# Gated scan and feed-forward on one core: second unit's spreads split between two queues, state copies on another engine, new order

## The chip, the cores and the metric

One core of a Trainium2 chip runs the whole program. The metric is the device time of one execution in microseconds. TensorE, VectorE, ScalarE, GpSimd and SyncE run their own instruction streams and wait for each other by semaphores; in the views they are PE (its weight loads PEld), DVE, ACT, POOL and SP. SP computes nothing here: it issues transfers.

## The reference

For 4 batches and 8 heads, a state of 48 x 48 complex numbers is decayed by a gate and fed with k and v at each of 768 steps; y is read out with q. The rows of y, 3072 tokens of 384, then go through a feed-forward layer of 2048 with a piecewise quadratic gate.

```python
for t in range(S):
    ar, ai = (a_re_n[:, :, t, :, None], a_im_n[:, :, t, :, None])
    new_re = ar * S_re - ai * S_im
    new_im = ar * S_im + ai * S_re
    kv = np.einsum('bhd,bhe->bhde', k[:, :, t], v[:, :, t])
    S_re, S_im = (new_re + kv, new_im)
    y[:, :, t] = np.einsum('bhd,bhde->bhe', q[:, :, t], S_re)
...
h = x @ w_in
g = np.where(pos, h, np.where(neg, 0.0, (h + beta) ** 2 / (4.0 * beta)))
return (g @ w_out).astype(np.float32)
```

(a_re_n and a_im_n are the gates, scaled to a size below 1; pos and neg are h >= 1 and h <= -1.)

## The kernel before

The tokens are cut into 12 units of 256 (3 of each batch), and a unit into 2 chunks of 128. Each unit passes through two stages. `gates(u)` makes running sums of the logarithms and angles of the gates (logarithm, exponential, arctangent and sine on ScalarE, the rest on VectorE; for units 0 and 1 the sums are matmuls of TensorE), multiplies k and q with them (the tile `kq`, and `x`: the "turn", two instructions of VectorE for units 0 and 1), and sends the two results from their rows to rows sorted by head: `spread`, five transfers for `x` and five for `kq`, into three tiles `hd0`, `hd1` (three heads each) and `hd2` (two heads). `attend(u)` then takes each chunk through visits of TensorE: the scores of all heads into two PSUM tiles, which VectorE masks into `am0` and `am1` (copy under a mask, "masked copy"); the transposes of k, which ScalarE copies to `kT`; the values (`am` times `V`, plus state times q from the second chunk on), which ScalarE copies to `xr`; and the products of k and v, which go to the state `st`. When a unit's values stand in `xr`, six small transfers move rows of two heads within it. `split` makes the two parts `xH` (ScalarE) and `xL` (VectorE) of `xr`, and `moe` runs the feed-forward part over a block of two units: `gemm1(f)` into `h`, the gate on ScalarE and VectorE (`s`, `g`, `gh`, `gl`), `gemm2(f)`. The first two f of block 0 run on one unit at a time. Each matmul of it is done three times, on upper and lower parts. The weights are decoded on the way: `raw_i` and `raw_o` are loaded, and VectorE and ScalarE make upper and lower parts; for the first three tiles TensorE forms the lower one (`rest`).

The order of the work is not found at run time: every operation is recorded with its engine and its cost, and `ORDER`, a written table of 2324 numbers, says in which order all are emitted. Each engine then runs its own in that order. `Plan.order` works out planned times from the costs; they are used for one thing only, the number of filler matmuls (`idle`) that `warm` puts ahead of a TensorE operation where the plan has a gap, up to the first one of `moe`. What an instruction waits for is found from the tiles that it reads and writes when it is emitted, not from the plan. Transfers take eight semaphores in turn, over all queues together; a transfer that takes a semaphore again waits until the one that had it before has landed.

In `attend`, `visit` records the parts of a visit one after the other, and the first of them carries what all of them read:

```python
last = pl.op("PE", cost, run, r=reads if n == 0 else r, w=[psum], glue=last)
```

In `gates`, `spread(g, e, t)` takes its engine from a table of which no unit makes use (`SPREADS = 0`), so SP issues all:

```python
eng = SPREAD[e] if u < SPREADS else "SP"
```

e = 1 is the spread of `x` and e = 0 that of `kq`, which comes second.

Of the kernel before, what the change touches and what calls it, by code (L numbers as in the profile page):

```python
# [15 lines left out]
ALU = mybir.AluOpType  # L16
# [7 lines left out]
HR = 2 * D  # L24
# [40 lines left out]
    0, 1, 11, 2, 192, 201, 219, 210, 42, 3, 28, 4, 106, 12, 151, 5, 13, 14, 6, 193, 7, 194, 15, 8,  # L65
    16, 195, 9, 17, 196, 10, 18, 197, 202, 20, 19, 198, 203, 21, 26, 22, 211, 24, 23, 27, 212, 25,
    30, 35, 204, 34, 213, 31, 220, 32, 46, 29, 45, 33, 221, 199, 38, 40, 47, 39, 225, 41, 48, 97,
    54, 36, 44, 49, 43, 98, 51, 50, 55, 52, 53, 99, 200, 57, 100, 60, 101, 56, 37, 102, 103, 61, 58,
    205, 59, 104, 107, 206, 62, 105, 65, 66, 214, 113, 63, 207, 64, 152, 208, 111, 226, 118, 222,
    153, 114, 227, 110, 154, 112, 67, 228, 223, 109, 69, 209, 68, 116, 229, 155, 71, 115, 73, 72,  # L70
    117, 215, 70, 74, 108, 230, 156, 75, 231, 224, 157, 237, 77, 166, 76, 158, 79, 81, 78, 159, 80,
    83, 160, 85, 119, 86, 161, 82, 216, 121, 84, 162, 87, 232, 164, 163, 95, 233, 165, 120, 88, 123,
    238, 125, 124, 92, 122, 126, 89, 239, 168, 127, 90, 167, 513, 129, 94, 128, 169, 93, 131, 130,
    91, 133, 170, 132, 540, 234, 135, 137, 136, 217, 134, 138, 171, 235, 139, 141, 297, 218, 240,
    140, 149, 142, 172, 241, 143, 173, 144, 298, 175, 146, 174, 236, 145, 305, 176, 317, 147, 306,
    242, 299, 318, 177, 148, 307, 300, 243, 96, 301, 329, 249, 541, 178, 308, 319, 302, 186, 320,
    303, 180, 542, 321, 309, 304, 179, 543, 310, 341, 311, 181, 188, 322, 312, 342, 182, 150, 323,
    244, 519, 330, 313, 245, 189, 343, 324, 187, 331, 314, 190, 246, 315, 353, 523, 325, 250, 354,
    517, 247, 316, 355, 191, 326, 332, 338, 183, 248, 327, 184, 340, 333, 544, 516, 365, 334, 185,
    328, 339, 545, 255, 251, 350, 518, 344, 522, 335, 351, 546, 515, 252, 366, 336, 514, 509, 547,  # L80
    345, 520, 511, 253, 337, 521, 346, 510, 363, 548, 254, 352, 356, 347, 364, 261, 549, 367, 348,
    555, 357, 524, 256, 526, 824, 550, 349, 362, 527, 512, 525, 374, 368, 551, 528, 358, 369, 257,
    554, 530, 359, 529, 532, 370, 258, 534, 371, 259, 533, 376, 553, 552, 262, 377, 360, 260, 378,
    557, 263, 379, 267, 389, 361, 372, 390, 531, 558, 264, 388, 380, 559, 375, 373, 381, 560, 387,
    265, 391, 382, 399, 392, 383, 536, 561, 393, 538, 401, 268, 394, 562, 402, 537, 556, 384, 386,
    564, 403, 563, 385, 400, 565, 395, 412, 566, 266, 413, 396, 269, 411, 273, 404, 414, 567, 405,
    415, 270, 406, 571, 398, 574, 397, 271, 410, 573, 407, 422, 416, 572, 568, 425, 417, 575, 569,
    423, 408, 578, 825, 272, 426, 577, 579, 424, 409, 539, 580, 427, 570, 418, 576, 434, 274, 279,
    826, 436, 419, 428, 275, 435, 429, 437, 276, 827, 438, 535, 277, 439, 828, 581, 420, 278, 829,
    280, 285, 830, 589, 421, 598, 582, 281, 591, 601, 430, 602, 831, 593, 440, 595, 431, 603, 447,  # L90
    832, 590, 604, 449, 441, 592, 605, 450, 833, 442, 597, 606, 608, 599, 443, 451, 600, 834, 282,
    444, 448, 596, 607, 835, 432, 461, 609, 446, 586, 283, 462, 585, 433, 838, 463, 587, 594, 837,
    584, 459, 286, 445, 891, 841, 610, 287, 836, 284, 842, 612, 611, 288, 291, 452, 614, 839, 843,
    464, 613, 616, 615, 289, 844, 460, 453, 618, 620, 619, 472, 617, 454, 471, 621, 845, 465, 455,
    622, 624, 846, 466, 290, 623, 892, 632, 292, 625, 467, 847, 626, 840, 458, 456, 630, 473, 848,
    631, 474, 583, 468, 457, 849, 475, 868, 293, 627, 485, 476, 850, 588, 486, 893, 294, 483, 856,
    628, 487, 852, 477, 857, 470, 478, 469, 858, 295, 484, 479, 855, 482, 851, 636, 629, 634, 496,
    871, 296, 480, 494, 861, 488, 481, 495, 859, 489, 853, 498, 854, 638, 490, 873, 637, 499, 635,
    894, 860, 497, 862, 491, 642, 895, 639, 863, 650, 492, 896, 877, 640, 651, 870, 493, 897, 643,
    878, 641, 500, 633, 875, 898, 876, 501, 899, 872, 502, 874, 503, 864, 900, 505, 869, 866, 507,  # L100
    865, 504, 901, 506, 879, 508, 867, 881, 880, 652, 902, 882, 644, 908, 903, 968, 904, 883, 645,
    646, 885, 884, 647, 653, 887, 648, 654, 889, 906, 655, 658, 907, 888, 659, 890, 910, 669, 649,
    660, 909, 656, 670, 661, 668, 911, 657, 666, 662, 667, 912, 905, 663, 678, 913, 664, 671, 680,
    672, 665, 681, 914, 677, 673, 682, 915, 679, 683, 674, 691, 916, 688, 675, 917, 692, 684, 918,
# [1686 lines left out]
```

## Time and profile before

| | us |
|---|---|
| median of 3 runs | 556.41 (556.22 to 556.45) |
| the profiled execution | 555.64 |
| its span, first to last instruction | 553.7 |
| PE busy | 543.3 |
| DVE busy | 434.0 |
| ACT busy | 390.2 |

The profiled execution is shorter than the median by 0.77 us; 1.94 us of it lie outside the span. All times in the rows are counted from the start of the span. The granted clock of TensorE was 1.00 in all 40 slices of the page. Idle time of DVE and ACT costs something only where PE waits behind it.

### The profile page before, as it was taken

Reading aid. Unit: us, or ns where it says so; the run is one execution under the profiler, and the core shown is the slowest. Engines: PE = TensorE matmul, PEld = TensorE weight load, DVE = VectorE, ACT = ScalarE, POOL = GpSimd, SP = SyncE. Lnnn points to the kernel's source line nnn. Section 1 sums busy time; section 2 is a strip of 40 time slices with the busy share of each in tenths; the row PEclk is TensorE's granted clock in tenths of the full one; section 3 lists DMA queues with packets and bytes.
Section 4 is the critical chain, followed back from the end, with each engine's and each line's share of the span. In section 5 each row is a group of like instructions: output and inputs, shape, how many; then the busy total and the mean of one; then the engine's idle time right before and its main releaser. Section 6 shows DMA issues by size and latency. Waiting matters only on the chain.

```text
span 553.7 us, 10884 instructions
## 1 busy us (share of the span) xinstructions
PE 543.3 (98%) x4255; PEld 459.0 (83%) x4255; DVE 434.0 (78%) x631; ACT 390.2 (70%) x634; POOL 4.1 (1%) x27
## 2 busy tenths in 40 slices
PE   7999999999999999999999999999999999999997
PEld 7878878888888888888888888888888888888885
DVE  6999999999899798896977887776887476454553
ACT  7896899989966767666755776555753455577875
POOL 2000000000000000000000000000000000000000
PEclk9999999999999999999999999999999999999999
DMA  8776564465451342542411532421534510077751
GB/s 343 305 209 250 193 199 186 122 210 185 135 195 52 87 141 70 188 126 76 156 57 47 181 114 54 165 60 37 187 98 120 179 56 9 24 262 240 265 178 60
DMA packets 28487, 80.58 MB, mean 146 GB/s; under 512 B 6160, under 2 KB 13200, under 8 KB 28432
## 3 DMA queue, kind: packets, MB, share of 16 engines
q1 hardware_dynamic: 28288, 79.72, 43.4%
q8 instruction: 34, 0.56, 0.4%
q14 instruction: 21, 0.17, 0.1%
q10 hardware_dynamic: 144, 0.13, 0.1%
HBM read 55.05 MB, written 4.72 MB: 108 GB/s over the span
## 4 chain that ended last, share of the span: by engine, by line
PE 87%; DVE 6%; ACT 2%; DMA 2%; issue 1%; SPq 1%; ACTq 0%; DVEq 0%
PE o L1371 36%; PE h L1294 35%; PE at L1119 5%; PE at L1163 3%; PE at L1171 3%; PE at L1091 2%; PE at L1062 2%; DMA ai<-in_art_dram 1%; SPq L474 1%; DVE kq L828 1%; DVE kq L962 1%; DMA xr<-xr 1%; DVE x L962 1%; ACT ai L690 1%; DVE x L711 0%
## 5 line engine op out<-in xcount | busy, mean ns | idle before, releaser
L1371 PE MATMUL o<-gh,wo 128*128 128x512 f32 x576 | 178.9, 392 | 0.0
L1294 PE MATMUL h<-xH,wi 128*128 128x512 f32 (+1 forms) x576 | 177.4, 389 | 0.3 <-DVE g L1338 0.2
L1371 PEld LDWEIGHTS o<-gh,wo 128*128 128x128 f32 x576 | 106.5, 188 | 22.2 <-issue 0.2
L1294 PEld LDWEIGHTS h<-xH,wi 128*128 128x128 f32 x576 | 105.7, 188 | 22.7 <-DVE g L1338 1.5
L1371 PE MATMUL o<-gl,wo 128*128 128x512 f32 x288 | 112.0, 389 | 0.0
L1294 PE MATMUL h<-xL,wi 128*128 128x512 f32 (+1 forms) x288 | 111.4, 387 | 0.2 <-DVE xL L1269 0.2
L1319 ACT ACTIVATE s<-h,cst 128x512 f32<-128x512 f32 x94 | 64.4, 687 | 59.7 <-PE h L1294 38.7
L1338 DVE TENSOR_TENSOR g<-h,s 128x512 f32<-128x512 f32 x94 | 64.7, 689 | 50.9 <-ACT s L1319 49.2
L1356 DVE TENSOR_TENSOR gl<-g,gh 128x512 fp32r<-128x512 f32 x96 | 65.9, 687 | 25.8 <-ACT gh L1352 25.0
L1352 ACT CAST gh<-g 128x512 fp32r<-128x512 f32 x96 | 59.1, 616 | 28.1 <-DVE g L1346 18.5
L1294 PEld LDWEIGHTS h<-xL,wi 128*128 128x128 f32 x288 | 54.1, 188 | 11.8 <-DVE xL L1269 0.6
L1371 PEld LDWEIGHTS o<-gl,wo 128*128 128x128 f32 x288 | 54.0, 188 | 11.4
L1346 DVE SCALAR_TENSOR_TENSOR g<-s,g 128x512 f32<-128x512 f32 x80 | 54.9, 687 | 1.2
L690 ACT ACTIVATE ai<-ai 128x768 f32<-128x768 f32 (+1 forms) x48 | 40.5, 846 | 10.9 <-DVE ai L704 5.4
L1131 DVE COPY_PREDICATED am<-tri,at 128x512 f32<-128x512 uint32 x44 | 32.4, 741 | 8.2 <-PE at L1119 8.1
L1119 PE MATMUL at<-hd 96*64 96x128 f32 (+1 forms) x704 | 35.8, 248 | 0.1
L773 DVE TENSOR_TENSOR_SCAN ai<-again,ai 128x768 f32<-128x768 uint8 x20 | 35.1, 1753 | 1.0 <-ACT ai L690 0.9
L1119 PEld LDWEIGHTS at<-hd 96*64 96x64 f32 x704 | 33.4, 137 | 1.2 <-issue 0.7
L1171 PE MATMUL at<-am,V 128*64 128x128 f32 x352 | 33.1, 273 | 0.1
L1163 PE MATMUL at<-hd,st 96*64 96x128 f32 x304 | 30.7, 278 | 0.0
L483 ACT ACT_TABLE_LOAD x23 | 29.5, 1283 | 0.4
L1068 ACT COPY kT<-at 128x384 f32<-128x384 f32 x36 | 16.8, 478 | 11.0 <-PE at L1062 10.9
(137 smaller groups left out, 650.6 us busy)
## 6 DMA issues: line engine op xcount, KB each, us to landing
chk<-in_wl_dram SPq DMA_DIRECT2D x16, 768.0 KB, 5.6
kq<-in_kq_dram SPq DMA_DIRECT2D x12, 768.0 KB, 6.2
ai<-in_ari_dram SPq DMA_DIRECT2D x10, 768.0 KB, 5.3
V<-in_v_dram SPq DMA_DIRECT2D x12, 576.0 KB, 5.4
raw_i<-in_wl_dram SPq DMA_DIRECT2D x8, 768.0 KB, 5.0
raw_o<-in_wl_dram SPq DMA_DIRECT2D x8, 768.0 KB, 5.6
hd<-kq SPq DMA_DIRECT2D x40, 144.0 KB, 2.3
hd<-x SPq DMA_DIRECT2D x40, 144.0 KB, 2.4
```

Of the source, the lines that this page charges most:

```text
L690: lambda: A_.activation(out(), src(), f, **kw),
L773: lambda: V_.tensor_tensor_scan(dst().rearrange("p j t -> p (j t)"), again, src().rearrange("p j t -> p (j t)"), 0.0, op0=ALU.mult, op1=AL ...
L1119: PE_.matmul(SC.get()[o : o + HC, i + e, HC * k :], chunk(h, c, 0, HC * k)[:, :HC], chunk(h, c, 1, HC * k), start=True, stop=True,)
L1163: PE_.matmul(o_, st.get().rearrange("p h e -> p (h e)")[:, lo : lo + 64], chunk(h, c, 1), start=True, stop=False,)
L1171: PE_.matmul(o_, V.get()[:, c, lo : lo + 64], ams[pr // 2].get()[:, 2 * (pr % 2) + e, :], start=st is None, stop=True,)
L1294: PE_.matmul(H.get()[:, lo:hi], weight["i", f // 2].get()[:, f % 2, part, sl], x.get()[:, j, lo:hi], start=j == 0 and n == 0, stop=j == NJ ...
L1319: lambda: A_.activation(SS.get(), H.get(), AF.Relu, bias=c_half, scale=-0.5 if spare else 0.5),
L1338: lambda: V_.tensor_tensor(G.get(), H.get(), SS.get(), op=ALU.max),
L1346: lambda: V_.scalar_tensor_tensor(G.get(), SS.get(), 1.0, G.get(), op0=ALU.min, op1=ALU.mult),
L1352: pl.op("ACT", act(T), lambda: A_.copy(GH.get(), G.get()), r=[G], w=[GH])
L1356: lambda: V_.tensor_tensor(GL.get(), G.get(), GH.get().bitcast(F32), op=ALU.subtract),
L1371: PE_.matmul(LAST.get() if half else PO[m].get()[:, ts], weight["o", f // 2].get()[:, f % 2, part, sl], g.get()[:, ts], start=(f == NF - h ...
```

## The change

Five transfers of unit 1 (the spreads of `kq`) are issued by ScalarE instead of SP. The first copy of each batch's state from PSUM is done by ScalarE instead of VectorE. For unit 0 each part of a visit is recorded with its own reads alone. The table `ORDER` is another one throughout.

```diff
-SPREADS = 0
-SPREAD = ("SP", "ACT")
...
-            eng = SPREAD[e] if u < SPREADS else "SP"
+            eng = "ACT" if u == 1 and not e else "SP"
...
             def tail():
                 if old is None:
-                    fn = lambda: V_.tensor_copy(ST.get(), DP.get()[:HR])
-                else:
-                    fn = lambda: V_.tensor_tensor(ST.get(), old.get(), DP.get()[:HR], op=ALU.add)
-                pl.op("DVE", dve(DM), fn, r=[DP] + ([old] if old else []), w=[ST])
+                    pl.op(
+                        "ACT",
+                        act(DM, psum=True),
+                        lambda: A_.copy(ST.get(), DP.get()[:HR]),
+                        r=[DP],
+                        w=[ST],
+                    )
+                    return
+                pl.op(
+                    "DVE",
+                    dve(DM),
+                    lambda: V_.tensor_tensor(ST.get(), old.get(), DP.get()[:HR], op=ALU.add),
+                    r=[DP, old],
+                    w=[ST],
+                )
...
-                last = pl.op("PE", cost, run, r=reads if n == 0 else r, w=[psum], glue=last)
+                last = pl.op("PE", cost, run, r=reads if n == 0 and u else r, w=[psum], glue=last)
...
 ORDER = [
-    0, 1, 11, 2, 192, 201, 219, 210, 42, 3, 28, 4, 106, 12, 151, 5, 13, 14, 6, 193, 7, 194, 15, 8,
...
+    0, 1, 11, 2, 192, 210, 201, 28, 106, 3, 219, 4, 42, 12, 151, 5, 13, 14, 6, 193, 7, 194, 15, 8,
...
```

All 2324 places of the table are open to the change; three of them matter to the text below.

The first place is the issue of unit 1's spreads. In SP's list before, all ten stand in a row behind unit 0's, `x` and `kq` mixed (line 474 is the issue of a transfer; `hd_364`, `hd_386` and `hd_356` are unit 1's three tiles, `x_157` and `kq_148` its `x` and `kq`; the semaphores named are those that a transfer waits for).

```order
L474 DMA hd_356<-x_157 16x512 [waits DMAHW7_49,DVE_49]
L474 DMA hd_356<-kq_148 16x512 [waits DMAHW0_49,DVE_49]
L474 DMA hd_364<-kq_148 48x1536 [waits DMAHW1_49]
L474 DMA hd_356<-x_157 32x1024 [waits DMAHW2_49]
L474 DMA hd_356<-x_157 16x512 [waits DMAHW3_49]
L474 DMA hd_386<-x_157 48x1536 [waits DMAHW4_49]
L474 DMA hd_356<-kq_148 32x1024 [waits DMAHW5_49]
```

In SP's list now (L472), only the five of `x` stand there, behind a weight load (L486; unit 1's tiles are now `hd_370`, `hd_385` and `hd_373`), and the first of them waits for semaphore 2, which ScalarE's first transfer has.

```order
L486 DMA raw_i_360<-in_wl_dram 128x1536 [waits DMAHW1_49,PE_49]
L472 DMA hd_370<-x_157 48x1536 [waits DMAHW2_49,DVE_49]
L472 DMA hd_373<-x_157 16x512 [waits DMAHW3_49]
L472 DMA hd_385<-x_157 48x1536 [waits DMAHW5_49]
L472 DMA hd_373<-x_157 32x1024 [waits DMAHW7_49]
L472 DMA hd_373<-x_157 16x512 [waits DMAHW1_49]
```

In ScalarE's list now, the five of `kq` stand between its computing instructions, two together and three one by one among the copies of `kT` (L1066), `xr` (L1192) and the state (L1102); L688 is a gate instruction, and the fifth follows one `kT` copy behind the last row shown.

```order
L472 DMA hd_370<-kq_155 48x1536 [waits DVE_49]
L472 DMA hd_385<-kq_155 48x1536 [waits DMAHW5_49]
L525 CAST wo_398<-raw_o_256 128x2x384 [waits DMAHW3_49,DVE_49]
L688 ACTIVATE ai_159<-ai_159 128x768 [waits DVE_49]
L1066 COPY kT_93<-at_111 128x384 [waits PE_49]
L1066 COPY kT_94<-at_109 128x384 [waits DVE_49,PE_49]
L688 ACTIVATE ai_159<-ai_159,cst 128x768 [waits Activation_49]
L1192 COPY xr_444<-at_110 128x4x128 [waits DVE_49,PE_49]
L472 DMA hd_373<-kq_155 16x512 [waits DMAHW4_49]
L1102 COPY st_466<-at_111 96x384 [waits PE_49]
L688 ACTIVATE x_351<-x_351,cst 128x768 [waits DVE_49]
L472 DMA hd_373<-kq_155 32x1024 [waits DMAHW6_49]
```

The second place is TensorE behind the transposes of unit 0's second chunk (L1062 is a transpose, L1119 a score, L1163 and L1171 the values). Before, the scores of unit 1 (`hd_1`) come next, and unit 0's values behind them.

```order
L1062 MATMUL at0_109<-ident_64,hd0_121 128x96
L1062 MATMUL at0_109<-ident_64,hd1_122 128x96
L1062 MATMUL at0_109<-ident_64,hd2_123 128x96 x2
L1119 MATMUL o0_112<-hd_1_364 64x128
L1119 MATMUL o0_112<-hd_1_386 64x128
```

Now unit 0's values follow (L1172 and L1180), then its products, and only then unit 1's scores.

```order
L1060 MATMUL at0_109<-ident_64,hd0_121 128x96
L1060 MATMUL at0_109<-ident_64,hd1_122 128x96
L1060 MATMUL at0_109<-ident_64,hd2_123 128x96 x2
L1172 MATMUL at1_110<-hd0_121,st_0_466 64x128
L1172 MATMUL at1_110<-hd1_122,st_0_466 64x128
L1180 MATMUL at1_110<-am0_82,V_0_260 64x128 x2
```

The third place is VectorE from the turns of unit 1 (L962, `x_1` and `kq_1`) to the masked copies of unit 0's first chunk (L1131). Before, the weight instructions (L503, L521, L512) stand behind both turns, and a gate instruction of unit 2 (L704) between the masked copies.

```order
L962 TENSOR_TENSOR kq_0_152<-kq_0_152,ai_0_135 128x1536
L962 TENSOR_TENSOR x_1_157<-kq_1_148,ai_1_137 128x1536
L962 TENSOR_TENSOR kq_1_148<-kq_1_148,ai_1_137 128x1536
L503 TENSOR_SCALAR y_o1_358<-raw_o1_270 128x768
L521 SCALAR_TENSOR_TENSOR raw_i2_144<-raw_i2_144 128x768
L512 SCALAR_TENSOR_TENSOR raw_o1_270<-raw_o1_270,y_o1_358 128x768
L521 SCALAR_TENSOR_TENSOR raw_o1_270<-raw_o1_270 128x768
L1131 COPY_PREDICATED am0_82<-tri_69,at0_109 128x512
L704 TENSOR_TENSOR ai_2_159<-ai_2_159 128x768
L1131 COPY_PREDICATED am1_83<-tri_69,at1_110 128x512
```

Now a weight instruction stands ahead of each turn of unit 1, and the two masked copies follow each other.

```order
L960 TENSOR_TENSOR kq_0_146<-kq_0_146,ai_0_135 128x1536
L510 SCALAR_TENSOR_TENSOR raw_o1_256<-raw_o1_256,y_o1_312 128x768
L960 TENSOR_TENSOR x_1_157<-kq_1_155,ai_1_137 128x1536
L519 SCALAR_TENSOR_TENSOR raw_i2_152<-raw_i2_152 128x768
L960 TENSOR_TENSOR kq_1_155<-kq_1_155,ai_1_137 128x1536
L519 SCALAR_TENSOR_TENSOR raw_o1_256<-raw_o1_256 128x768
L702 TENSOR_TENSOR ai_2_159<-ai_2_159 128x768
L1140 COPY_PREDICATED am0_82<-tri_69,at0_109 128x512
L1140 COPY_PREDICATED am1_83<-tri_69,at1_110 128x512
```

The same instructions stand there in both but for the places named; the masked copies of unit 0's second chunk follow each other now too, and in unit 1's first chunk a weight instruction (L519) stands between them.

## Rows read from the trace of the kernel before

**Rows 1.** Two stretches: busy us of each engine, granted clock, DMA share, GB/s.
```profile
30.00:50.00 20.00, 18.44 (x273) 16.18 (x273) 19.83 (x25) 16.21 (x25) 0.00 (x0) 1.00 0.79 263
70.00:545.00 475.00, 475.00 (x3565) 399.21 (x3566) 366.89 (x529) 330.22 (x548) 0.00 (x0) 1.00 0.40 130
```

**Rows 2.** TensorE in order of time: start, us, engine, line, what [idle before].
```profile
36.00 2.13 PE L1119 MATMUL at<-hd 96*64 96x128 f32 x32
...
39.98 1.09 PE L1171 MATMUL at<-am,V 128*64 128x128 f32 x16
...
44.94 1.57 PE L1119 MATMUL o<-hd 96*64 96x128 f32 x31 [0.71 <-DMA hd<-x]
46.33 0.29 PE L1163 MATMUL at<-hd,st 96*64 96x128 f32 x1
...
49.18 0.88 PE L1062 MATMUL o<-ident,hd 96*128 96x96 f32 x8
...
50.46 1.09 PE L1171 MATMUL o<-am,V 128*64 128x128 f32 x16
...
58.54 1.16 PE L1441 MATMUL idle<-tri,ident 128*128 128x128 f32 x8
...
60.36 0.40 PE L1294 MATMUL h<-xH,wi 128*128 128x256 f32 x2
...
60.72 0.40 PE L1294 MATMUL h<-xH,wi 128*128 128x256 f32 x2
...
67.46 0.62 PE L1294 MATMUL at<-xH,wi 128*128 128x512 f32 x2
...
68.14 0.62 PE L1294 MATMUL at<-xH,wi 128*128 128x512 f32 x2
...
69.90 0.73 PE L1294 MATMUL h<-xH,wi 128*128 128x512 f32 x2 [0.24 <-DVE g L1338]
```

**Rows 3.** VectorE in order of time, same columns.
```profile
32.79 1.76 DVE L962 TENSOR_TENSOR kq<-kq,ai 128x1536 f32<-128x1536 f32 x1
...
39.20 0.73 DVE L1131 COPY_PREDICATED am<-tri,at 128x512 f32<-128x512 uint32 x1
...
49.41 0.73 DVE L1131 COPY_PREDICATED am<-tri,o 128x512 f32<-128x512 uint32 x1
...
54.93 0.74 DVE L1131 COPY_PREDICATED am<-tri,o 128x512 f32<-128x512 uint32 x1
...
59.13 0.95 DVE L1269 TENSOR_TENSOR xL<-xr,xH 128x768 fp32r<-128x768 f32 x1
```

**Rows 4.** ScalarE in order of time, same columns.
```profile
48.52 0.56 ACT L1183 COPY xr<-at 128x512 f32<-128x512 f32 x1
...
57.39 0.83 ACT L1262 CAST xH<-xr 128x768 fp32r<-128x768 f32 x1 [1.25 <-DMA xr<-xr]
```

**Rows 5.** The tiles hd, 27 to 50 us: issues min/median/max ns, landing.
```profile
L474 SPq DMA_DIRECT2D hd<-kq x10: 514/588/1430, 31.0 to 40.2; - x10
...
DMA to landing us min/median/max: 2.2/3.2/4.1
```

**Rows 6.** The end: issues of the output (ns), and ScalarE's copies.
```profile
L474 SPq DMA_DIRECT2D out_dram<-ob x2: 394/394/395, 548.1 to 549.1; - x2
L474 ACTq DMA_DIRECT2D out_dram<-ob x1: 381/381/381, 548.6 to 548.6; - x1
547.46 1.64 ACT L1412 COPY ob<-o 128x512 f32<-128x512 f32 x3 [1.71 <-PE o L1371]
```

**Rows 7.** SP's waits in all: us, times, longest.
```profile
SPq L474 <- DMA hd<-kq: 9.8, 5, 3.7
```

**Rows 8.** Transfers issued in the first 62 us: KB, median us to landing.
```profile
hd<-kq SPq DMA_DIRECT2D x4, 32.0 KB, 2.5
```

**Rows 9.** Copies out of PSUM by line: busy us, mean ns | idle before.
```profile
L1101 DVE COPY st<-at 96x384 f32<-96x384 f32 x3 | 1.6, 546 | 0.2 <-PE at L1091 0.2
L1068 ACT COPY kT<-at 128x384 f32<-128x384 f32 x36 | 16.8, 478 | 11.0 <-PE at L1062 10.9
```

268 rows, old and new, of the table ORDER are left out of this document.

## The prediction

> **What bounds the kernel now.** I read the stretches first, then TensorE in order of time, and then who it waited for. From 70 to 545 us TensorE is busy for 475.00 of 475.00 us at the granted clock 1.00, the upper of its two levels (2.4 GHz) [rows 1]; the reader is to see that nothing done there on another engine can show as time, unless it opens a gap. Both orders hold the same matmuls: 2043 of the feed-forward part, 1241 of gates and attention, 12 of the weights' rests; only the fillers go from 80 to 76, and they stand in idle time. So the end moves by as much as the last idle moment before 70 us moves. That is the first group of gemm1 for f = 4, at 69.90, behind a wait of 0.24 us for a `g` of VectorE [rows 2].
>
> Ahead of it lies the prologue. There TensorE waits, and these are the places [rows 2]: scores of unit 0 from 36.00 for 2.13 us, though the same 32 matmuls take 1.57 us at 44.94; 0.71 us before 44.94 for spreads of unit 1; fillers until 50.46; fillers from 58.54 until the feed-forward part starts; and then a first group that ends only at 60.36, because `xL` is made from 59.13 to 60.08 [rows 3]. From 60.36 to 69.90 there are 9.54 us for 11 groups of 256 columns (0.36 us each, 60.36 to 60.72) and 6 of 512 (0.68 us, 67.46 to 68.14): 3.96 + 4.08 = 8.04 us of work, 1.50 us of waiting [rows 2].
>
> VectorE is full in that time (19.83 of 20 us between 30 and 50), ScalarE is not (16.21 of 20) [rows 1]. ScalarE stands 1.25 us before it makes `xH` at 57.39, waiting for the moves `xr<-xr` [rows 4].
>
> **Part by part.**
>
> *The waits of unit 0's visits.* The line changes what the planner believes, not what an instruction waits for. In the order before, the first matmul of the scores already waits for hd0's and the second for hd1's transfers, and only the ones on hd2 for hd2's; in the trace the scores start at 36.00 and stretch. So the edit by itself is worth 0; it acts through the table alone. No cover is needed for it.
>
> *VectorE up to the first values.* The values of unit 0's first chunk start at 39.98, right behind the second masked copy (39.20, 0.73 us) [rows 2, 3]. In the new table the two masked copies follow each other, and what stands ahead of them is the same work, less one copy of `state`. With VectorE nearly full, the saving lies between 0 (if the spreads of unit 0 land later than now) and some 0.7 us (the 0.17 us of idle time in [rows 1], and what dependent steps that now have other work between them lose beside it, which I estimate at 0.5). I take 0.4: values at 39.58.
>
> *Unit 0 finishes before unit 1 starts.* From 39.98 to the end of the second chunk's transposes at 44.23 (44.94 less 0.71) are 4.25 us of work [rows 2]; it now ends at 43.83. Then come unit 0's last values and products (46.33 to 49.18, 2.85 us), which need nothing of unit 1, and unit 1's scores (44.94 to 46.33, 1.39 us) behind them. I add 0.2 us for the masked copy just ahead: values 44.03, products end 46.88, scores 46.9 to 48.3, if unit 1's spreads have landed; all this was done at 49.18 before.
>
> *Have they landed?* On VectorE the turns of unit 1 come later: one weight instruction of 128x768 stands ahead of each of the two (0.95 us, the price of `xL`, which has the same size [rows 3]), so the `kq` turn ends at 34.55 + 1.9 = 36.45 at most. ScalarE then issues two moves, 0.59 us each by SP's price for the same moves [rows 5]. At the end of the trace the two queues issue the same output transfer in 0.38 and 0.39 us, and ScalarE's issue, at 548.6, runs beside its copies (547.46 to 549.10) [rows 6]: an issue costs ScalarE between 0 (hidden behind a running instruction) and 0.59 us; for the first two, which wait for VectorE with nothing behind them, I take 0.59, for the other three 0.2. Eight semaphores are handed round over both queues, and SP's first `x` move of unit 1 now waits for the semaphore of ScalarE's first move, so it waits for that landing: 36.45 + 3.2 (median) = 39.65 [rows 5]. That such waits are real shows in SP's own: 9.8 us in 5 times on `hd<-kq` [rows 7]. Five issues later, at 42.0, the last `x` move goes out and lands at 45.2, or 46.1 with the longest landing, 4.1 us. ScalarE's last move stands behind a `kT` copy of unit 0's second chunk, at about 44.3; with 2.5 us for a move of 32 KB [rows 8] it lands at 46.8. Needed at 46.9: no wait, but no room either. Behind those issues on ScalarE stand the `kT` copies, the state copy and `xr`, for which TensorE and SP's moves wait; behind SP's wait stand the load of `raw_o` and of the next `kq`, needed after 49 us.
>
> *The first state copy.* It leaves VectorE (0.55 us each, four in the kernel) [rows 9] and costs ScalarE its own 384 columns; the nearest row is the `kT` copy of 384 columns, 0.48 us [rows 9]. VectorE is full and ScalarE has 3.79 us idle in 20, so it is hidden; without that cover it costs 0.48 us. Two lie in the prologue.
>
> *Unit 1.* Its first values wait for a masked copy again: before, it ended at 50.14 and they started at 50.46. Now the first masked copy can start at about 47.85, a weight instruction (0.95) stands between, the second ends at 50.05, values at 50.15: 0.3 us gained of the 0.9 at the scores, because VectorE takes the rest back. At the second chunk no weight instruction stands between any more, only the state addition, and VectorE's second masked copy moves from 54.93 to about 54.1 [rows 3]. The same four instructions follow up to `xL`, so `xL` goes from 59.13 to 58.3 and is done at 59.25; TensorE's fillers are over at 58.54 - 0.3 + 0.7 = 58.9. First group done at 59.55 instead of 60.36: **0.8 us**.
>
> *`xH` and the stretch to 69.90.* The `xr` copy of unit 0 was at 48.52, behind two exponentials; now it comes right behind the values, at about 46.0. The six moves and the loads between them took from 49.08 to 57.39; the same 8.3 us from 46.5 end at 54.8, plus some 0.5 us for a larger load that now stands among them. `xH` is only reached after unit 1's `kT` copies, at about 55.3, so its 1.25 us wait goes. Of the 1.50 us of waiting behind 60.36 this gives back between 0 and all; I take a third, **0.5 us**, as ScalarE stays nearly full there.
>
> Sum: 0.8 + 0.5 = 1.3 us. The profiled execution took 555.64 us (span 553.7), so it would be 554.3; the median of the runs is 556.41, so 555.1.
>
> *A rule of the skill.* In [rows 6] SP issues at 548.1 and 549.1 and ScalarE at 548.6: the trace has no two issues at the same time, so it does not show whether they disturb each other. The Trainium skill, "Perfetto Trace Analysis", section "DMA Instruction — HWDGE (DVE, Sync)", says that the block which generates descriptors is shared and locked for one issuer at a time; no run here shows it. By it an issue of ScalarE would have to queue behind one of SP's when both are ready, and with one such turn lost, 0.59 us, the time would be 555.7; its chance lies in the first rival below.
>
> **Rivals.**
>
> *The landing of unit 1 eats the gain.* Place: unit 1's first scores, 46.9. With every landing at 4.1 us, ScalarE's last move lands at 44.3 + 4.1 = 48.4, 1.5 us late; one lost turn at an issue (0.59) adds to it. For it: the hand-over of semaphores between the queues, and three links in a row. Against it: the small moves took 2.5 us. The 0.8 go, a part of the 0.5 stays: 556.1, within 0.2%. The line on reads alone doing nothing, and the table being worth nothing, ends here too (556.4).
>
> *ScalarE becomes late (slower).* One of SP's moves took 1.43 us to issue [rows 5]. If ScalarE's five took that, they cost 5 x 1.43 - 5 x 0.59 = 4.2 us more, against 1.3 us gained; that is 2.9 us later if nothing of it lies in idle time and, as I take it, 1.7 us with a good part there: 558.1. It decides from 0.59 + 1.3 / 5 = 0.85 us an issue (the gain is gone) and 0.59 + 2.4 / 5 = 1.07 us (slower by 0.2%). Against it: 0.38 to 0.39 on either queue in [rows 6], median 0.59.
>
> *A new gap after 70 us.* All later blocks are reordered, and now no gap exists to be saved; one transfer that comes late by its own 2.5 us [rows 8] costs 1.2 us net of the gain: 557.6. Against it: three quarters of that time VectorE has room (366.89 of 475 us) [rows 1].
>
> **How the numbers follow.** A change of 0.2%, 1.1 us, is about what a measurement of this kernel can tell. Forecast 0.55 (555.1; its own range 553.9 to 555.3, the lower end with all 1.50 us given back and 0.2 more at the start); landing or nothing 0.32 (555.3 to 557.5, mostly 556.1); late ScalarE 0.08 and a gap later 0.05 (slower). So faster 0.55, same 0.32, slower 0.13. The range 553.9 to 556.7 leaves out the slower cases and the far end of the forecast.
>
> **What would show it.** Right: unit 0's values run straight on behind its second transposes, before any wait for `hd`; SP's first `x` move of unit 1 waits for `hd<-kq`; `xH` no longer waits for `xr<-xr`; the first group of f = 4 stands near 68.6; from there to the end TensorE has no gap. Wrong: a wait of more than 1 us for `hd` at unit 1's scores; ScalarE issues of 0.9 us or more; `xL` not before 59; or a gap on TensorE after 70 us.

## The result, and the profile after

The changed kernel takes 561.38 us (561.05 to 563.01, 6 runs) against 556.21 us; the ratio is 1.01, 95% interval 1.0086 to 1.0113. It is slower by 5.2 us, where 1.3 us less was forecast. The profiled execution has a span of 559.6 us (553.7 before).

The first view is busy time by stretches of the changed kernel (columns as in [rows 1]).

```profile
46.00:50.00 4.00, 1.61 (x46) 1.49 (x43) 1.62 (x2) 2.06 (x3) 0.00 (x0) 1.00 0.75 216
50.00:57.00 7.00, 7.00 (x81) 6.66 (x79) 5.29 (x6) 3.84 (x6) 0.00 (x0) 0.51 0.99 376
57.00:60.00 3.00, 3.00 (x44) 2.42 (x40) 2.12 (x5) 2.25 (x6) 0.00 (x0) 1.00 0.02 6
70.00:545.00 475.00, 474.03 (x3555) 397.14 (x3555) 366.11 (x527) 329.79 (x547) 0.00 (x0) 1.00 0.41 133
```

From 46 to 50 TensorE and VectorE are idle for more than half of the time, ScalarE for nearly half, while the transfers run; behind it the granted clock is 0.51, the lower of TensorE's two levels. From 70 us on nearly nothing is idle, as in [rows 1]. So the loss is made ahead of 70 us again. TensorE in order of time shows where.

```profile
39.36 1.09 PE L1180 MATMUL at<-am,V 128*64 128x128 f32 x16
...
45.68 1.08 PE L1089 MATMUL at<-V,kT 128*64 128x48 f32 x32
49.15 1.92 PE L1128 MATMUL o<-hd 96*64 96x128 f32 x32 [2.39 <-DMA hd<-x]
...
53.38 1.98 PE L1180 MATMUL o<-am,V 128*64 128x128 f32 x16
55.14 1.68 PE L1089 MATMUL o<-V,kT 128*64 128x48 f32 x30
...
56.81 1.62 PE L1128 MATMUL o<-hd 96*64 96x128 f32 x31
...
63.95 0.47 PE L1303 MATMUL h<-xH,wi 128*128 128x256 f32 x2
...
74.36 0.73 PE L1303 MATMUL h<-xH,wi 128*128 128x512 f32 x2 [0.49 <-DVE g L1347]
```

Unit 0 does what was forecast: values at 39.36, products done at 46.76. Then unit 1's scores wait 2.39 us for the transfer `hd<-x`. Its values come at 53.38 instead of 50.46 [rows 2], 2.92 us late; what follows up to 56.81 runs at the lower clock; and the first group of f = 4 stands at 74.36 instead of 69.90, 4.46 us late. The span is 5.9 us longer. Of the other 1.4 us the trace shows 0.5 behind it, in three waits of TensorE for VectorE's `g` and `gl` up to 111 us; no row accounts for the rest.

Why is `hd<-x` late? SP's list and ScalarE's list in order of time (an engine's name with q is its issuing of transfers):

```profile
35.05 0.53 SPq L486 DMA_DIRECT2D raw_i<-in_wl_dram  x1
43.22 3.85 SPq L472 DMA_DIRECT2D hd<-x  x5
```

```profile
36.34 1.26 ACTq L472 DMA_DIRECT2D hd<-kq  x2
37.70 0.90 ACT L525 CAST wo<-raw_o 128x768 fp32r<-128x768 f32 x1 [1.36 <-DVE raw_o L519]
...
39.97 0.94 ACT L688 ACTIVATE ai<-ai,cst 128x768 f32<-128x768 f32 x1
40.51 0.53 ACTq L472 DMA_DIRECT2D hd<-kq  x1
```

SP's own waits up to 60 us (us, times, longest) begin with this row:

```profile
SPq L472 <- DMA hd<-kq: 7.6, 1, 7.6
```

The issues of 34.9 to 37.5 us and that of SP's last `x` move (KB, median us to landing):

```profile
raw_i<-in_wl_dram SPq DMA_DIRECT2D x1, 768.0 KB, 6.0
hd<-kq ACTq DMA_DIRECT2D x2, 288.0 KB, 6.8
...
hd<-x SPq DMA_DIRECT2D x1, 32.0 KB, 3.5
```

The load of 768 KB goes out at 35.05 and lands at 41.1, 6.0 us later. ScalarE's first two moves go out at 36.34 and 37.00 and land 6.8 us later, the first at 43.16. SP's first `x` move has the semaphore of that one, and SP waits 7.6 us for it, until 43.22; the last of the five is issued at 46.02 and lands at 49.5. Before, unit 1's last move landed at 44.9 (issued at 40.82, 4.1 us [rows 5]).

What the queues moved (packets, MB, share of 16 engines; q1 is SP's, q10 ScalarE's) from 36.3 to 38, from 38 to 39 and from 40 to 41:

```profile
q1 hardware_dynamic: 85, 0.46, 80.0%
...
q1 hardware_dynamic: 54, 0.28, 85.2%
q10 hardware_dynamic: 14, 0.09, 27.3%
...
q10 hardware_dynamic: 51, 0.22, 69.1%
q1 hardware_dynamic: 2, 0.01, 3.0%
```

ScalarE's moves, issued from 36.34, have no packet before 38. About 1 us passes without any load as well (the first transfer of the kernel before is issued at 0.85 and has its first packet behind 1.8). From 38 to 39 ScalarE's queue moves 0.09 MB beside SP's 0.28, and from 40 on it has the transfer engines nearly to itself: most of its two moves goes out as SP's queue runs empty.

### The profile page after: what moved, and what is told of

It reads as the page before. It is cut to its first block, busy times and chain, and to the rows that moved or that the text cites. A ratio compares the mean times of both kernels' runs of the same rounds, so it can differ in the third digit from the quotient of the medians.

```text
span 559.6 us, 10886 instructions
## 1 busy us (share of the span) xinstructions
PE 547.1 (98%) x4247; PEld 461.6 (82%) x4247; DVE 431.7 (77%) x627; ACT 391.1 (70%) x638; POOL 4.1 (1%) x27
## 3 DMA queue, kind: packets, MB, share of 16 engines
q1 hardware_dynamic: 28048, 78.93, 42.2%
## 4 chain that ended last, share of the span: by engine, by line
PE 81%; DVE 10%; DMA 5%; issue 2%; SPq 1%; ACT 0%; DVEq 0%
PE o L1380 33%; PE h L1303 32%; PE at L1128 5%; PE at L1172 3%; PE at L1180 3%; PE at L1089 2%; DMA raw_i<-in_wl_dram 2%; PE at L1060 2%; DMA raw_o<-in_wl_dram 1%; SPq L472 1%; DVE kq L826 1%; DMA ai<-in_art_dram 1%; DVE ai L771 1%; DMA hd<-x 1%; DVE g L1347 1%
## 5 line engine op out<-in xcount | busy, mean ns | idle before, releaser
L1303 PEld LDWEIGHTS h<-xL,wi 128*128 128x128 f32 x288 | 54.1, 188 | 11.5 <-DVE xL L1278 0.3
L688 ACT ACTIVATE ai<-ai 128x768 f32<-128x768 f32 (+1 forms) x48 | 40.3, 844 | 9.5 <-DVE ai L879 7.0
L1180 PE MATMUL at<-am,V 128*64 128x128 f32 x352 | 32.9, 273 | 0.1
L1172 PE MATMUL at<-hd,st 96*64 96x128 f32 x304 | 30.5, 278 | 0.1
L688 ACT ACTIVATE ai<-ai,cst 128x768 f32<-128x768 f32 x24 | 22.5, 937 | 3.4 <-DVE ai L900 3.0
```

The costliest lines, as they stand in the source:

```text
L688: lambda: A_.activation(out(), src(), f, **kw),
L1172: PE_.matmul(o_, st.get().rearrange("p h e -> p (h e)")[:, lo : lo + 64], chunk(h, c, 1), start=True, stop=False,)
L1180: PE_.matmul(o_, V.get()[:, c, lo : lo + 64], ams[pr // 2].get()[:, 2 * (pr % 2) + e, :], start=st is None, stop=True,)
L1303: PE_.matmul(H.get()[:, lo:hi], weight["i", f // 2].get()[:, f % 2, part, sl], x.get()[:, j, lo:hi], start=j == 0 and n == 0, stop=j == NJ ...
```

## The experiments

**Theory A**: the load delays ScalarE's first move, and the shared semaphore hands the delay to SP. **Rival B**: what ScalarE issues lands late by itself. **Rival C**: the load delays every move behind it, whoever issues it. **Rival D**: the later part of the new order loses too. Filler matmuls that the planner would have added ahead of unit 1's scores were left out unless said. All ratios are to the kernel before.

| run | us (median) | ratio, interval |
|---|---|---|
| e1_sp_issues | 563.69 | 1.0145, 1.0130 to 1.0160 |
| e2_pool_issues | 561.13 | 1.0085, 1.0067 to 1.0102 |
| e4_filled | 562.63 | 1.0124, 1.0110 to 1.0137 |
| e5_load_late_sp | 560.65 | 1.0078, 1.0054 to 1.0102 |
| e6_load_late_act | 561.66 | 1.0111, 1.0089 to 1.0132 |
| e7_before_load_early | 561.43 | 1.0089, 1.0063 to 1.0115 |
| e8_filled10 | 561.14 | 1.0097, 1.0076 to 1.0118 |
| e9_before_act | 556.56 | 1.0012, 1.0000 to 1.0024 |
| e10_before_state | 557.09 | 1.0017, 1.0000 to 1.0033 |
| e11_before_head | 558.44 | 1.0044, 1.0028 to 1.0059 |
| e12_best_sp | 557.25 | 1.0023, 1.0007 to 1.0038 |
| e13_xl_first | 558.14 | 1.0036, 1.0023 to 1.0049 |
| e14_sp_nofill | 565.53 | 1.0169, 1.0155 to 1.0182 |
| e15_act_repaired | 557.88 | 1.0027, 1.0015 to 1.0039 |
| e16_xh_next | 558.15 | 1.0040, 1.0025 to 1.0055 |

### Who issues the moves (e1, e14, e2)

```diff
-            eng = "ACT" if u == 1 and not e else "SP"
+            eng = "SP"                                       # e1, e14
+            eng = "POOL" if u == 1 and not e else "SP"       # e2
```

e1_sp_issues: 

> The changed kernel with unit 1's five kq moves issued by SP again, the new order kept. Theory A (a weight load of 768 KB ahead of ScalarE's first move makes it land after 6.8 us, and SP's first x move waits for that landing, because it has the same semaphore): without the second queue SP's first x move goes out at about 35.7 instead of 43.2, all ten are issued by about 43, TensorE's wait of 2.39 us before unit 1's scores goes, the granted clock stays 1.00, and the time is 555 to 556 us. Rival B (a transfer issued by ScalarE lands late whatever lies ahead of it): the same here. Rival C (the load alone holds up every spread that stands behind it, whoever issues it): the wait stays at 1 us or more, 558 to 561 us.

Measured 563.69. The planner had put 22 filler matmuls (5.18 us) ahead of unit 1's scores, so TensorE's start there says nothing. The moves do: SP's first `x` move goes out at 35.72, and it lands at 42.2. e14 leaves the fillers out.

e14_sp_nofill: 

> The changed kernel with SP issuing all ten moves of unit 1, the load of 768 KB still ahead of them, and without the 22 filler matmuls that the planner put ahead of unit 1's scores in the first run of that kind (5.18 us). Theory C (the load alone delays what stands behind it): the x and kq moves that unit 1's first scores need land at 46.5 to 47 as there, the last two kq moves behind the second load at 52.5; TensorE waits 3 to 5 us in unit 1's scores and the time is 561 us or more. Theory A (without the second queue no delay): no wait of over 0.5 us, 555 to 557 us.

Measured 565.53. TensorE in order of time:

```profile
47.69 1.31 PE L1128 MATMUL o<-hd 96*64 96x128 f32 x24 [0.32 <-DMA hd<-kq]
53.56 1.10 PE L1128 MATMUL o<-hd 96*64 96x128 f32 x8 [4.56 <-DMA hd<-kq]
```

Theory A falls: without ScalarE's queue and its semaphores it is 4 us worse, and the wait is now for SP's last `kq` moves, which stand behind the next loads too.

e2_pool_issues: 

> The changed kernel with the five kq moves of unit 1 issued by GpSimd, whose transfers take semaphores of their own, so that no move of SP waits for one of them; the load stays where it is. Theory A: SP's first x move at about 35.7, no wait of more than 0.5 us before unit 1's scores, 555 to 556.5 us. Rival B: as A. Rival C: the wait stays at 1 us or more, 558 us or more.

Measured 561.13. The moves issued from 34.9 to 46.6:

```profile
hd<-x SPq DMA_DIRECT2D x1, 128.0 KB, 11.1
hd<-kq POOLq DMA_DIRECT2D x1, 128.0 KB, 11.0
...
hd<-kq POOLq DMA_DIRECT2D x2, 32.0 KB, 10.6
```

No move of SP waits for a semaphore of the other queue here, all are out by 39.3, and the last land at 49.5 all the same, where they landed with the change. The semaphore only moves the wait from the transfer to its issue. The scores did not wait as long as C said (they started at 48.07) and gemm1 starts sooner (61.53 against 63.95), so the equal time has another place: behind 70 us TensorE now stands idle for 3.7 us.

```profile
70.00:545.00 475.00, 471.29 (x3541) 394.81 (x3540) 363.69 (x524) 326.90 (x544) 0.00 (x0) 1.00 0.40 131
```

Why it does was not tried; what e2 shows is the landing.

### How large the load is (e3)

```diff
+        if k == 3:
+            nc.gpsimd.memset(flat[:, DM:], 0)
+            nc.sync.dma_start(flat[:, :DM], wl[k].bitcast(U32)[:, :DM])
+            return
         nc.sync.dma_start(flat, wl[k].bitcast(U32))
```

e3_small_load: 

> The changed kernel with the one weight load ahead of unit 1's moves cut from 768 to 192 KB (three quarters of that weight tile are set to zero by GpSimd, so that part of the weights is left out). ScalarE still issues the kq moves and SP still shares the semaphores. Theory A: ScalarE's first move lands after some 3.5 us instead of 6.8, SP's first x move goes out at about 40, the wait of 2.39 us shrinks to under 0.5, the clock stays 1.00, and the time is 555 to 556.5 us. Rival B: ScalarE's first move still takes 6 us or more and the time stays at 560 to 561 us. Rival C: as A.

With this weight cut, the program does not end with its fast part but goes on with the general path that it keeps for other inputs (14624.69 us in all), so only the prologue is read. SP's wait for ScalarE's first move:

```profile
SPq L472 <- DMA hd<-kq: 3.9, 1, 3.9
```

SP's first `x` move goes out at 39.66 instead of 43.22, as expected. So a quarter of the load makes half of the wait; rival B falls. TensorE waited all the same before the last part of unit 1's scores:

```profile
51.06 1.00 PE L1133 MATMUL o<-hd 96*64 96x128 f32 x8 [3.14 <-issue]
```

The row names no transfer. SP came to the next load (768 KB, at 43.03) ahead of ScalarE's last move (44.19), and I take it that this move landed late behind it; e6 shows the like with the transfer named.

### Where the load stands (e7, e5, e6)

```diff
 ORDER of before (231: load of raw_i; 108 to 118: unit 1's moves; some others left out)   # e7
-    208, 111, 118, 114, 110, 112, ... 108, 75, 231, 237, ...
+    208, 231, 111, 118, 114, 110, 112, ... 108, 75, 237, ...
```

e7_before_load_early: 

> The kernel before with one number of its table moved: the load of raw_i (768 KB) is issued ahead of unit 1's ten moves instead of behind them. Nothing is issued by ScalarE. Theory C: the ten moves land some 4 to 5 us later (last at 49 to 50 instead of 44.9), unit 1's scores wait that long, and the time goes to 560 to 562 us. Theory A (it takes the semaphore shared with ScalarE): the moves share the engines with the load and land at most 1 to 2 us later, 556 to 558 us.

Measured 561.43. One number of the old table moved costs as much as the whole change. SP and TensorE in order of time:

```profile
34.79 0.35 SPq L470 DMA_DIRECT2D raw_i<-in_wl_dram  x1
```

```profile
49.04 2.90 PE L1101 MATMUL o<-hd 96*64 96x128 f32 x32 [3.53 <-DMA hd<-x]
```

Six fillers of the planner (1.53 us) stand ahead of that wait. The last move is issued at 44.02 and lands at 49.0, 4.1 us later than before, with no transfer on ScalarE's queue. That is rival C, for SP's own queue; that it holds for another queue's moves is shown by e2 and e6.

```diff
 ORDER of the change                                                            # e5, e6
-    223, 231, 215, 109, ...  224, 237, 77, 76, 232, ... 85, 166, 116, 160, 87, 86, 117, 233, ...
+    223, 215, 109, ...  117, 231, 237, 166, ...  120, ... 122, 232, 233, 238, ... 239, 234, ...
```

e5_load_late_sp: 

> The changed kernel with SP issuing all ten moves of unit 1 and with the three loads (raw_i, raw_o, kq) that stand ahead of or between them moved behind them, as in the kernel before; the instructions that decode this weight on VectorE stand behind unit 1's first masked copies. Theory C (the load alone delays every move behind it by its own 5 us): the last move of unit 1 lands at about 45 instead of 49.5, unit 1's scores start at about 46.8 without a wait, first gemm1 at about 60, f = 4 at 69 to 70, 555 to 556.5 us. Theory D (the new order loses time behind the prologue too, whatever unit 1's landing does): no wait at 46.8, but gaps of 1 us or more between 60 and 120, 557 us or more.

Measured 560.65; its six runs spread from 558.74 to 562.32, and the profiled one is the longest. Unit 1 lands at 44.3 and its scores run from 46.28 without a wait, as C says, yet the time hardly falls. A row of TensorE and one of VectorE:

```profile
56.73 0.55 PE L1042 MATMUL o<-ident,hd 96*128 96x96 f32 x4 [2.25 <-DVE am L1122]
```

```profile
52.54 1.76 DVE L808 TENSOR_TENSOR kq<-kq,x 128x1536 f32<-128x1536 f32 x1 [1.55 <-ACT ai L670]
```

VectorE stands 1.55 us before `kq<-kq,x` of unit 2, and what ended last is not the engine that the row names: the load of that `kq` (issued at 43.87) lands at 52.36. The masked copy that TensorE needs stands behind it. A second wait, for the next transfer, has taken the place of the first, and behind 70 us TensorE waits 3.0 us for `g` and `gl`, where before it waited for nothing.

e6_load_late_act: 

> As the one before, but with ScalarE issuing the five kq moves as in the change. SP has no more work then between its fifth move (about 42.5) and the loads, and ScalarE's last two moves come at 42.6 and 43.9. Theory C: SP issues the loads at about 42.5, so ScalarE's last moves land behind 768 KB again, at about 48, and TensorE waits 1 to 3 us before the last third of unit 1's scores: 557 to 560 us. If ScalarE's issue costs nothing once the load is out of the way: as the one before, 555 to 556.5 us.

Measured 561.66. ScalarE's last move (43.72) meets the load that SP issued at 43.04 and lands at 49.2; TensorE waits 1.61 us before the last third of the scores, as expected, and VectorE's wait comes behind it.

### The lower clock (e4, e8)

```diff
+        n += 21 if i == 119 else 0      # e4; 10 in e8: filler matmuls ahead of unit 1's scores
         if "over" not in idle and n > 0:
```

e4_filled: 

> The changed kernel with 21 filler matmuls more ahead of unit 1's first scores, which fill TensorE's idle 2.39 us and change nothing else. If the granted clock of 0.50 from 50.6 to 57 follows from that idle stretch: the scores start where they did (about 49.2), the clock stays 1.00 from 50 to 60, and what TensorE did at half clock there comes about 2 to 3 us sooner, so 558.5 to 559.5 us. If the clock falls for another reason, or if the other engines set the pace behind 50 us anyway: 561 us.

Measured 562.63. A filler matmul takes 0.235 us here and not half of it, so 21 of them lasted 4.96 us and held up the scores themselves; nothing follows from the time.

e8_filled10: 

> The changed kernel with 10 filler matmuls (0.235 us each, as the 21 of the run before took 4.96 us) ahead of unit 1's first scores: they fill 2.35 of the idle 2.39 us and end before the scores could start. If the lower clock follows from the idle stretch: clock 1.00 from 50 to 60, values of unit 1 about 1 us sooner, first gemm1 about 2 us sooner (62 instead of 63.95), 559 to 560 us. If it costs nothing, because the other engines set the pace there: 561 to 561.5 us with the clock at 1.00.

Measured 561.14. TensorE in order of time, and its stretch from 50 to 60 as in the first view:

```profile
46.67 2.50 PE L1451 MATMUL idle<-tri,ident 128*128 128x128 f32 x20
49.10 1.56 PE L1128 MATMUL o<-hd 96*64 96x128 f32 x32
...
52.32 1.09 PE L1180 MATMUL o<-am,V 128*64 128x128 f32 x16 [0.38 <-DVE am L1140]
...
54.16 1.52 PE L1128 MATMUL o<-hd 96*64 96x128 f32 x31
...
62.39 0.47 PE L1303 MATMUL h<-xH,wi 128*128 128x256 f32 x2
...
72.17 0.73 PE L1303 MATMUL h<-xH,wi 128*128 128x512 f32 x2 [0.73 <-DVE g L1347]
```

```profile
50.00:60.00 10.00, 8.65 (x147) 7.58 (x145) 8.85 (x12) 6.93 (x12) 0.00 (x0) 1.00 0.68 257
```

With the idle stretch filled the clock stays 1.00 (0.66 from 50 to 60 with the change). From the values to the second scores it is 1.84 us (52.32 to 54.16) instead of 3.43 (53.38 to 56.81): the lower clock cost 1.6 us at this place, and gemm1 starts 1.56 us sooner. But the time is that of the change: waits of 0.73 us at 71.4 and 1.35 us at 90.7, both for VectorE's `g`, take it back. VectorE waited there for weight loads, 2.6 us for `raw_i` and 1.1 for `raw_o`. SP issues one `raw_i` at 64.88 us here, at 66.89 with the change and at 62.94 before; and the next `raw_i` at 81.07, 83.07 and 74.92: the loads stay late in SP's list when the scores no longer are.

### The other edits, alone (e9, e10)

```diff
-            eng = SPREAD[e] if u < SPREADS else "SP"
+            eng = "ACT" if u == 1 and not e else "SP"        # e9, with the table of before
...
+                if old is None:                              # e10, with the table of before
+                    pl.op("ACT", act(DM, psum=True), lambda: A_.copy(ST.get(), DP.get()[:HR]), r=[DP], w=[ST])
+                    return
```

e9_before_act: 

> The kernel before with its own table and one edit alone: ScalarE issues the five kq moves of unit 1 (the same filler matmuls as before). The loads stand behind SP's five x moves, which go out about 3 us earlier than now. If what delays unit 1 is a load that is issued ahead of its moves: ScalarE's last moves (issued at 38 to 41) meet SP's loads (from about 38 on) and land 1 to 4 us later than 44.9; 557 to 560 us. If an issue by ScalarE is nearly free and only the new table puts a load ahead: 555.5 to 556.7 us.

e10_before_state: 

> The kernel before with its own table and one edit alone: the first copy of each batch's state on ScalarE. By the prediction it is hidden: 555.5 to 556.5 us. If ScalarE is late there by 0.48 us with VectorE not the one that waits: 556.5 to 557 us.

Measured 556.56 and 557.09. Neither gains; each costs between nothing and 0.24% or 0.33%. For the state copy that is 0 to 1.8 us, which does not tell a hidden copy from one that costs its 0.48 us; its profile has a wait of 1.4 us of TensorE for `am` in the prologue that the one before has not. In e9 the loads stand behind SP's last move, and unit 1's last move lands at 44.65.

### The later part of the new order (e11)

```diff
 ORDER of before up to gemm1 of f = 4, then all that is left as it stands in the new table
-    ..., 353, (rest of before)
+    ..., (rest of the new table)
```

e11_before_head: 

> The edits of the kernel before, with a table that is the one of before up to the first group of gemm1 for f = 4 and from there has everything that is left in the sequence of the new table. If the new table loses only in the prologue: no gap behind 70, 555.5 to 556.7 us. If its later part loses too (theory D): gaps between 70 and 120 and 557 us or more.

Measured 558.44: between 0.28 and 0.59% are lost (rival D). Not all of it lies in the later part: in the profiled execution f = 4 stands at 70.98 instead of 69.90, though the table is the same up to there; unit 1's last move landed at 45.7 instead of 44.9. One profile can differ from another by such an amount. Behind 70 TensorE is idle for 1.8 us. A row of VectorE and one of TensorE:

```profile
85.30 0.56 DVE L485 TENSOR_SCALAR y_i<-raw_i 128x768 uint32<-128x768 uint32 x1 [2.10 <-DMA raw_i<-in_wl_dram]
```

```profile
89.70 0.72 PE L1276 MATMUL h<-xH,wi 128*128 128x512 f32 x2 [1.35 <-DVE g L1320]
```

The load of the next `raw_i` is issued at 79.04, where the kernel before has it at 74.92.

### Taking the new waits away, one by one (e12, e13, e15, e16)

SP issues all; the loads are late as in e5; then instructions are moved out of the way, step by step.

```diff
 sequence of the operations (167, 239: unit 2's kq, a weight; 134: second masked copy; 298: xL; 218: cast of rest_o; 299: next xH)
-    167, 239, 234, 132, ... 134, ...
+    132, ... 134, 167, 239, 234, ...      # e12, and at most 4 fillers ahead of gemm1
+    297, 298, 234, 235, 171, ...          # e13: xL ahead of 234, 171, 240
+    138, 218, ... 140, ... 142, 235, ...  # e15
+    142, 143, 144, 235, 299, 300, ...     # e16
```

e12_best_sp: 

> The new table with the loads behind unit 1's moves (as in the run with the loads late, SP issuing all), and with VectorE's work on the kq of unit 2 and on the weights, which waited for those loads, behind the second masked copies of unit 1's second chunk instead of ahead of them; at most 4 filler matmuls ahead of gemm1. If a wait of VectorE for a load took the place of TensorE's wait for unit 1: the 2.25 us at 54.5 go, first gemm1 at 57.5 to 59.5, 554.5 to 556.5 us. If the weights' loads set the end anyway: the gaps between 70 and 92 grow by as much, 558 to 560 us.

e13_xl_first: 

> As the last run with the new table and the loads late (557.25), with xL of unit 0 made on VectorE right behind xH, ahead of three weight and gate instructions (4.9 us of VectorE's work stood between them, and TensorE waited 2.64 us for xL). If what was left of the loss is that place of xL: TensorE's attention part ends at 57.4 as there, gemm1 runs on from 57.5 to 58 with its xL, f = 4 at 68 to 69.9, and the time is 554.5 to 556.3 us. If what is set aside (the scan of unit 2, the weights) is needed as soon: a gap of the same size opens between 60 and 92 and the time stays at 557 us or more.

e15_act_repaired: 

> As the run with xL first, with two casts moved in ScalarE's sequence: that of the rest of wo, for which TensorE waited 5.05 us, ahead of xH; and that of wi, which waits for VectorE, behind the copies of xr of unit 1. If the waits of the last three runs are one chain after the other (each one repaired shows the next), attention ends at 57.2 again, the six moves of xr of unit 1 start near 57.6 instead of 59, TensorE waits 1 to 2 us for the next xH, f = 4 stands at 68.5 to 69.9, and the time is 555 to 556.5 us. If a bound behind 70 (weight loads) sets the end, a gap opens there and it stays at 557 us or more.

e16_xh_next: 

> As e15, with the next xH (the first chunk of unit 1) ahead of three casts and gate instructions of ScalarE, and its xL ahead of VectorE's gate instructions. The moves that this xH needs landed at 60.24 in e15, xH came at 63.26, TensorE waited 4.06 us for it. If sequences alone are what is left of the loss: the wait falls to 1.5 to 2.5 us (TensorE is ready at 59.6), the clock stays 1.00, f = 4 at 68.5 to 70, and the time is 555 to 556.3 us, that of the kernel before or less. If transfers behind 70 set the end: the gap of 0.47 us at 88.8 grows to 1.5 us or more, and it is 557 us or more.

Measured 557.25, 558.14, 557.88 and 558.15. TensorE's largest wait behind 56 us in e12, e13 and e15:

```profile
61.84 0.38 PE L1285 MATMUL h<-xL,wi 128*128 128x256 f32 x1 [2.64 <-DVE xL L1260]
```

```profile
62.90 0.79 PE L1285 MATMUL h<-xH,wi 128*128 128x256 f32 x2 [5.05 <-ACT wo L535]
```

```profile
63.70 0.79 PE L1285 MATMUL h<-xH,wi 128*128 128x256 f32 x2 [4.06 <-ACT xH L1253]
```

and TensorE's waits in e16, summed:

```profile
PE h L1285 <- ACT xH L1253: 3.5, 2, 2.7
PE h L1285 <- DVE xL L1260: 0.5, 1, 0.5
```

e12 takes back 4.1 of the 5.2 us. Attention is done at 57.4 there, where the fillers of before begin at 58.54 [rows 2]. That 1.1 us would be the gain of the reorder (e11 shows that one profile can differ from another by as much, but all four have it, 57.2 to 57.4). None of the four kept it: each wait that was taken away showed the next, on VectorE or ScalarE, the clock fell again from 60 to 70 us (0.83 in e12, e15 and e16, 0.66 in e13, against 1.00 before), and f = 4 stands between 71.50 and 73.79. The expectations of e15 (a wait of 1 to 2 us) and e16 (the clock stays 1.00) were missed. The time stays 0.2 to 0.4% above the kernel before. In e16 no wait is left behind 70 us (475.00 of 475 us busy), so what is left is in the prologue alone. No version beat the kernel before; that none can is not shown.

## Why the prediction was wrong

**The step that failed** is *Have they landed?*, and in it the sentence that SP's first `x` move waits "for that landing: 36.45 + 3.2 (median) = 39.65". That it waits was right, and so was the time of ScalarE's issue (36.34). The landing took 6.82 us, so it was 43.16; the last `x` move landed at 49.5 instead of 45.2 to 46.1. The 3.2 us are the median of the moves in [rows 5], and between 23.29 and the last of those (40.82) SP issued no load. In the new order one stands ahead, and it was shown ahead of SP's moves and then costed at nothing. In the trace of before three such loads were there to price it: `raw_i`, `raw_o` and `kq`, issued at 41.50, 42.14 and 42.58, landed 5.1, 6.3 and 8.5 us later, one behind the other. e7 shows that its place alone is worth the loss, with no second queue; e3 shows it by its size; e14 and e2 that neither SP's nor GpSimd's queue avoids it.

The Trainium skill says it in one sentence: by "Trainium Kernel Development and Optimization", section "Key Constraints", transfers issued on different queues share the same 16 DMA engines, so that issuing from several engines saves issue time only. e2 agrees (SP's and GpSimd's queues in use, last landing at 49.5 as with SP's and ScalarE's). This rule speaks against the change, and should have been one of the rivals.

**The rival** "the landing of unit 1 eats the gain" had the place, but not the cause: it priced slow landings of 4.1 us and a lost turn at an issue, with no load in it, and had ScalarE's last move late (48.4; it landed at 47.8), where SP's last `x` move was (49.5). It was mis-sized too: 1.5 us late where it was 2.39, and 556.1 where it was 561.4. It let the wait take back the gain and no more. But VectorE stood as long, for the scores that it masks:

```profile
50.09 0.73 DVE L1140 COPY_PREDICATED am<-tri,o 128x512 f32<-128x512 uint32 x1 [2.44 <-PE o L1128]
```

The next load was late too (e5: 2.25 us), the clock fell and took 1.6 us at first (e8), and SP's later loads, late in their turn, hold up the feed-forward part behind 70 us (e8, and e11 without the late landing). Which of these holds the last microsecond depends on which is taken away, so their sizes don't add up to 5.2, and how the 5.2 us divide between them stays open.

**By the other steps.** Unit 0 finishing first: right (46.76 for 46.88). VectorE up to the first values: right (39.36 for 39.58). ScalarE's issue: right; three of its five issues lie beside running instructions (40.51 in 39.97 to 40.91), the first two in a wait for VectorE, and the rival "ScalarE becomes late" didn't happen. In the new order ScalarE's issue even helps by 4 us (e14 against the change). The state copy: between nothing and 0.33%, so not decided (e10). Unit 1's second masked copy at 54.1: it came at 59.05, behind `kq<-kq,x` and the late scores. A new gap behind 70 us: small with the change (0.49 us at most), but real in the later part of the table (e11: 1.35 us at 89.7). The argument against it misread [rows 1]: 366.89 of 475 us is what VectorE is busy, so it has room for a quarter of the time, and in the first 30 us none, as this stretch of the kernel before shows:

```profile
70.00:100.00 30.00, 30.00 (x243) 25.07 (x243) 30.00 (x45) 28.17 (x44) 0.00 (x0) 1.00 0.49 171
```

The weight given to it was too low. That recording unit 0's reads part by part is worth 0 by itself was not tried.

## What to carry to other kernels

When a reorder moves a large load ahead of small transfers, price the small ones with the load's own time, whichever queue issues them (here the first landed 2.1 us behind the load, from another queue); the landing times of the old order hold only for the old neighbours. A wait that lies ahead of several engines is not paid once: look which instruction stands behind it on each engine, and what that one waits for next. And where two engines and the transfers are all nearly full, a gap that one table closes opens somewhere else; count what each engine has to do up to the point from which one engine is always busy, and don't expect that point to come sooner than the fullest of them allows.

## What was not expected of the hardware

- ScalarE's queue got little beside SP's: of its two moves of 288 KB it had moved nothing by 38 us and 0.09 MB by 39, 2.7 us after the first issue, while SP's moved 0.74 MB from 36.3 to 39. Behind a quarter of the load (e3) it had moved 0.12 MB by 38.
- GpSimd's issues of moves took 0.49 to 0.63 us (e2), about as long as SP's there (0.52 to 0.61), and the last move landed at 49.5 as with ScalarE.
- An issue of SP beside one of ScalarE took 0.75 us (43.79, against 43.89 on ScalarE) instead of 0.52 to 0.59. The Trainium skill, "Perfetto Trace Analysis", section "DMA Instruction — HWDGE (DVE, Sync)", says that the block which generates descriptors is shared and held by one issuer at a time; no whole turn of 0.59 is lost here, and the 0.16 us can't be put down to it, as SP's issue at 44.59 also took 0.75 us with none of ScalarE beside it.
- The clock fell to the lower level after 2.39 us in which TensorE was idle, after 2.25 us in e5, and within an idle stretch of 3.53 us in e7; with the first of these stretches filled by fillers (e8) it stayed at the upper one.
